# Joining the 64-row matmuls of two FFN parts, with five PSUM banks in one pool, in an mLSTM cell followed by a squared-ReLU FFN

## The chip, the cores and the metric

One core of one Trainium2 chip. The metric is the device time of one execution in microseconds (us). All runs quoted here are of the fast state; the records show a granted TensorE clock of 0.988 to 0.991 over the span. A 2% change of the time counts as faster or slower.

## The reference

```python
# attention: mLSTM cell, batch 4, 8 heads, 768 steps, head size 40
for t in range(S):
    m_new = np.maximum(f_gate[:, :, t] + m, i_gate[:, :, t])
    f_stab = np.exp(f_gate[:, :, t] + m - m_new)
    i_stab = np.exp(i_gate[:, :, t] - m_new)
    C = f_stab * C + i_stab * einsum('bhd,bhe->bhde', vt, kt)
    n = f_stab * n + i_stab * kt
    y[:, :, t] = sigmoid(o_gate) * (C @ qt) / maximum(abs(n . qt), 1)
# FFN on x = (3072 tokens, 320): w_in (320, 2048), w_out (2048, 320)
h = np.maximum(x @ w_in, 0.0)
out = h * h @ w_out
```

The kernel computes attention in tiles of 128 steps (24 tiles) and the FFN in groups of 256 tokens (12 groups). The FFN's first product has a contraction of 320 rows: 128 + 128 + 64.

## The kernel before

An FFN group is done in four parts. Each part makes four blocks of 128 hidden columns: sixteen 128-row matmul instructions (an f32 matmul stands as two instructions in the trace), then eight 64-row ones. The latter come in pairs, one in rows 0 to 63 of the array and one in rows 64 to 127, each pair writing two different banks.

```python
    ps_at = ctx.enter_context(tc.tile_pool(name="ps_at", bufs=3, space=PSUM))
    ps_h = ctx.enter_context(tc.tile_pool(name="ps_h", bufs=3, space=PSUM))
    ps_o = ctx.enter_context(tc.tile_pool(name="ps_o", bufs=2, space=PSUM))
    ...
    def ffn1(g, pp):
        ...
        hs = [ps_h.tile([P, 2, WG], F32, name="h_ps") for _ in range(2)]
        for i in range(2):
            for n in range(2):
                fb = 4 * pp + 2 * n + i
                for a in range(2):
                    nc.tensor.matmul(                                        # line 460, 128 rows
                        hs[i][:, n, :], lhsT=w_in[:, a, fb * P : (fb + 1) * P], rhs=xT[:, a, :],
                        start=(n == 0 and a == 0), stop=False,
                    )
        for n in range(2):
            for i in range(2):
                rows = slice(i * KR, (i + 1) * KR)                           # KR = 64
                nc.tensor.matmul(                                            # line 467, 64 rows
                    hs[i][:, n, :], lhsT=w_in2[rows, 2 * pp + n, :], rhs=xT[rows, 2, :],
                    start=False, stop=(n == 1),
                )
        st["half"] = hs, ...
    ...
    for n, (which, g, i) in enumerate(parts):    # which 1: first product of group g, part i
        s, at = 6 + n // 4, n % 4                # which 2: second product of group g, step i
        if at == 0:
            do(score, s)          # scores of tile s: 40-row matmuls in pairs, then P_sb on VectorE
        if at == 1:
            attend_on(s)          # hi, dC, hp on TensorE, then x_sb on VectorE
        ...
        if at == 3:
            do(turn_rows, s)      # x_sb -> xT
            do(transposes, s + 1) # k, q -> kT (copied by ScalarE), qT
        if which == 1:
            ffn1(g, i)
            relu_half()           # ScalarE, PSUM -> r_sb
            square_half()         # VectorE, r_sb -> g2
        elif g == 0:
            ffn2(g, *divmod(i, 2))
        else:
            ffn2_fast(g, i)       # two banks X and Y over four steps
        ...
        if at == 2:
            do(weigh_on, s + 1)   # ScalarE: eight exponentials of the next tile (line 325)
```

Sets of four of `which` 1 and 2 take turns, so each tile of attention goes with one set. In line numbers below, L460, L467, L547 and so on are of the kernel before; in the changed kernel the same lines stand a little lower (L461, L472, L555).

## Time and profile before

| | kernel before |
|---|---|
| time, median | 584.4 us (583.93 to 585.96, 3 runs; a fourth, later, makes it 584.85) |
| span of the profiled run | 582.2 us |
| TensorE busy | 98% |
| VectorE, ScalarE, GpSimd busy | 54%, 34%, 17% |
| 64-row matmuls (L467) | 384 instructions, 48 blocks of 8 |

A row of the page's costliest groups gives line, engine, operation, tile written and read, shapes, count, busy time and the mean of one instruction, then the idle time of that engine just before. Here are the two rows of the 64-row block: its matmuls and its weight loads.

```profile
L467 PE MATMUL h_ps<-xT,w_in 64*128 64x256 f32 x384 | 54.5, 402 | 0.0
L467 PEld LDWEIGHTS h_ps<-xT,w_in 64*128 64x128 f32 x384 | 33.1, 186 | 18.0 <-issue 15.2
```

The matmul row has no idle time before it at all, yet the weight-load row has 18 us, 15.2 of it "issue", that is, waiting for nothing the profile shows. This is how lost time looks on a TensorE that counts as busy: a matmul record lasts longer (0.38 us for the 256 columns) than the distance to the next start (0.216), so the later start after a change of shape (0.309) leaves no gap between matmul records, and only the weight loads show one, 0.33 us each time. That gap marks the place and is not the price: from start to start the way into a block costs 0.20 us (0.309 + 0.320 against 2 x 0.216).

### The profile page before, as it was taken

The numbers are of one execution on the slowest core, as the hardware profiler recorded it, in microseconds if no ns is written. First come the engines' busy times: TensorE is split into PE (matmuls) and PEld (weight loads), VectorE is DVE, ScalarE is ACT, GpSimd is POOL, SyncE is SP. The second block draws the span as 40 slices with busy tenths as digits, with TensorE's granted clock in tenths as the row PEclk, the third lists the DMA queues.
The fourth block names the chain that finished last, engine by engine and source line by source line (L and its number), as shares of the span: only waits on it lengthen the run. The fifth ranks groups of instructions, "written<-read, shape, count | busy, mean of one in ns | idle before, by whom it ended". The sixth has DMA issues, their size and how long they took to land.

```text
span 582.2 us, 9724 instructions
## 1 busy us (share of the span) xinstructions
PE 567.7 (98%) x3878; PEld 497.6 (85%) x3879; DVE 312.9 (54%) x602; ACT 197.6 (34%) x486; POOL 97.0 (17%) x113
## 2 busy tenths in 40 slices
PE   9988899969999999999999999999999999999997
PEld 5876788857789989989988988988987998988997
DVE  8689988656374364353364365355365355334441
ACT  3868665351333223414213415204225213112000
POOL 3455433132012020101110220100210200000000
PEclk9998999979999999999999999999999999999999
DMA  9997997822124233321431432141321000000000
GB/s 195 224 210 157 162 199 163 166 70 46 47 46 76 66 47 64 77 46 46 95 45 38 88 64 59 36 92 37 46 61 36 1 24 2 1 24 0 24 24 23
DMA packets 130909, 42.60 MB, mean 73 GB/s; under 512 B 101072, under 2 KB 127696, under 8 KB 130864
## 3 DMA queue, kind: packets, MB, share of 16 engines
q1 hardware_dynamic: 130768, 41.79, 34.7%
q8 instruction: 30, 0.49, 0.4%
q10 hardware_dynamic: 96, 0.20, 0.1%
q14 instruction: 15, 0.12, 0.1%
HBM read 37.95 MB, written 4.03 MB: 72 GB/s over the span
## 4 chain that ended last, share of the span: by engine, by line
PE 89%; DVE 6%; ACT 2%; issue 1%; POOL 1%; POOLq 0%; DVEq 0%; ACTq 0%
PE o_ps L547 29%; PE h_ps L460 26%; PE h_ps L467 8%; PE hp L399 6%; PE tp L362 4%; PE o_ps L493 3%; PE tp L349 3%; PE hi L385 3%; PE dC L392 3%; DVE mag L197 1%; PE tp L444 1%; ACT W_sb L325 1%; DVE mag L198 1%; PE idle L615 1%; PE A_ps L301 1%
## 5 line engine op out<-in xcount | busy, mean ns | idle before, releaser
L460 PE MATMUL h_ps<-xT,w_in 128*128 128x256 f32 x768 | 177.9, 385 | 1.1 <-ACT xT L445 1.1
L460 PEld LDWEIGHTS h_ps<-xT,w_in 128*128 128x128 f32 x768 | 143.0, 191 | 24.4 <-issue 4.0
L486 DVE TENSOR_TENSOR g<-r_sb 128x512 f32<-128x512 f32 x96 | 64.8, 716 | 90.4 <-ACT r_sb L479 90.4
L479 ACT ACTIVATE r_sb<-h_ps 128x512 f32<-128x512 f32 x96 | 52.0, 593 | 175.0 <-PE h_ps L467 174.6
L547 PE MATMUL o_ps<-w_out,g 128*128 128x160 f32 x528 | 76.9, 302 | 0.0
L547 PEld LDWEIGHTS o_ps<-w_out,g 128*128 128x128 f32 x528 | 72.5, 190 | 1.3 <-issue 0.3
L325 ACT ACTIVATE W_sb<-A_bc,b_T 128x128 f32<-128x128 f32 x176 | 53.8, 390 | 6.4 <-POOL A_bc L310 6.4
L467 PE MATMUL h_ps<-xT,w_in 64*128 64x256 f32 x384 | 54.5, 402 | 0.0
L547 PE MATMUL o_ps<-T,S 128*128 128x160 f32 x352 | 51.6, 300 | 0.0
L547 PEld LDWEIGHTS o_ps<-T,S 128*128 128x128 f32 x352 | 49.0, 190 | 0.1
L467 PEld LDWEIGHTS h_ps<-xT,w_in 64*128 64x128 f32 x384 | 33.1, 186 | 18.0 <-issue 15.2
L336 POOL TENSOR_TENSOR vw<-va,W_sb 128x328 f32<-128x328 f32 x20 | 15.4, 768 | 191.7 <-ACT W_sb L325 186.7
L399 PE MATMUL hp<-va,P_sb 128*128 128x41 f32 x368 | 44.1, 281 | 0.0
L399 PEld LDWEIGHTS hp<-va,P_sb 128*128 128x128 f32 x368 | 42.9, 192 | 0.0
L563 DVE TENSOR_TENSOR y_sb<-y_sb,o_ps 128x160 f32<-128x160 f32 x33 | 10.6, 321 | 55.1 <-PE o_ps L547 55.1
L418 POOL TENSOR_TENSOR C_sb<-C_sb,Cd 128x328 f32<-128x328 f32 x16 | 14.4, 898 | 132.9 <-DVE C_sb L410 132.8
L374 DVE TENSOR_TENSOR P_sb<-tp,W_sb 128x512 f32<-128x512 f32 x46 | 29.5, 684 | 12.3 <-PE tp L362 11.7
L563 DVE TENSOR_TENSOR y_sb<-o_ps,y_sb 128x160 f32<-128x160 f32 x22 | 7.1, 325 | 53.9 <-PE o_ps L547 31.1
L362 PEld LDWEIGHTS tp<-qT,kT 40*128 40x128 f32 x384 | 25.0, 195 | 11.8 <-ACT kT L353 7.1
L362 PE MATMUL tp<-qT,kT 40*128 40x128 f32 x384 | 28.5, 290 | 6.7 <-ACT kT L353 5.1
L572 ACT COPY y_sb<-o_ps 128x160 f32<-128x160 f32 x11 | 3.2, 292 | 70.8 <-PE o_ps L547 70.8
L349 PE MATMUL tp<-ident,kq 128*128 128x128 f32 x192 | 25.1, 274 | 1.6 <-DVE num L405 1.6
(98 smaller groups left out, 674.5 us busy)
## 6 DMA issues: line engine op xcount, KB each, us to landing
A_bc<-a_rows SPq DMA_DIRECT2D x22, 512.0 KB, 4.2
raw<-in_moe_w_out_dram SPq DMA_DIRECT2D x16, 320.0 KB, 3.3
raw<-in_moe_w_in_dram SPq DMA_DIRECT2D x8, 512.0 KB, 5.7
kq<-in_k_dram SPq DMA_DIRECT2D x24, 160.0 KB, 4.2
kq<-in_q_dram SPq DMA_DIRECT2D x24, 160.0 KB, 4.8
va<-in_v_dram SPq DMA_DIRECT2D x24, 160.0 KB, 4.1
og<-in_o_gate_dram SPq DMA_DIRECT2D x24, 160.0 KB, 3.9
out_dram<-y_sb SPq DMA_DIRECT2D x24, 160.0 KB, 1.8
```

What stands on the lines that cost most here:

```text
L325: nc.scalar.activation(d["W"][:, i * n + h, :], A[i][:, h, :], AF.Exp, bias=b_T[:, b, c, i * n + h : i * n + h + 1],)
L349: nc.tensor.transpose(tp[:, j, :], d["kq"][:, i, 2 * j : 2 * j + 2, :].rearrange("p h d -> p (h d)"), ident[:],)
L362: nc.tensor.matmul(sc[i][:, j, :], lhsT=d["kT"][rows, j, :], rhs=d["qT"][rows, j, :], start=True, stop=True,)
L374: nc.vector.tensor_tensor(t, d["sc"][i], d["W"][:].rearrange("p (j two) t -> p j two t", two=2)[:, :, i, :], op=ALU.mult,)
L385: nc.tensor.matmul(hi[:, 2 * j : 2 * j + 2, :].rearrange("p h d -> p (h d)"), lhsT=d["qT"][:, j, :], rhs=C[:, j].rearrange("p h d -> p (h ...
L399: nc.tensor.matmul(hp[:, h, :], lhsT=d["P"][h % 2][:, h // 2, :], rhs=d["va"][:, h, :], start=True, stop=True,)
L460: nc.tensor.matmul(hs[i][:, n, :], lhsT=w_in[:, a, fb * P : (fb + 1) * P], rhs=xT[:, a, :], start=(n == 0 and a == 0), stop=False,)
L467: nc.tensor.matmul(hs[i][:, n, :], lhsT=w_in2[rows, 2 * pp + n, :], rhs=xT[rows, 2, :], start=False, stop=(n == 1),)
L479: nc.scalar.activation(rs[-1][:], h[:], AF.Relu)
L486: nc.vector.tensor_tensor(g4[:, :, i, :], r[:], r[:], op=ALU.mult)
L547: nc.tensor.matmul(to, lhsT=lhsT[:, p], rhs=rhs[:, p, :], start=(start and p == 0), stop=(p == NPAIR - 1), skip_group_check=True,)
L563: add = lambda to, a, b: nc.vector.tensor_tensor(to, a, b, op=ALU.add)
```

## The change

The intent is to go to the 64-row shape half as often: the 64-row matmuls of parts 0 and 1 are issued together after part 1's 128-row ones, those of parts 2 and 3 after part 3's. Two parts are then open at once and hold four banks. As the FFN's first product had three banks and the second product two, the two pools become one of five, in tile 7, before the fourth group (group 3). The relus and squares of the first part of a pair move behind the joined block with those of the second.

```diff
+    banks = ExitStack()
+    ps_h = banks.enter_context(tc.tile_pool(name="ps_h", bufs=3, space=PSUM))
+    ps_o = banks.enter_context(tc.tile_pool(name="ps_o", bufs=2, space=PSUM))
...
-    def ffn1(g, pp):
+    def ffn1_main(g, pp):
...                                            # the 128-row matmuls, unchanged
+    def ffn1_rest(g, pp, hs):
...                                            # the 64-row matmuls, unchanged
+    def ffn1(g, pp):
+        ffn1_main(g, pp)
+        ffn1_rest(g, pp, st["half"][0])
...
-            st["o_ps"] = ps_o.tile([P, W], F32, name="o_ps")[:, :DM]
+            st["o_ps"] = ps_h.tile([P, W], F32, name="h_ps")[:, :DM]
...                                            # X and Y of ffn2_fast likewise from ps_h (no longer swapped by g)
         if n == 4:
             ...
+            banks.close()
+            ps_h = ctx.enter_context(tc.tile_pool(name="ps_h", bufs=5, space=PSUM))
...
-        if which == 1:
+        if which == 1 and g < 3:
             ffn1(g, i)
             relu_half()
             square_half()
+        elif which == 1:
+            ffn1_main(g, i)
+            if i % 2 == 0:
+                held = st["half"]
+            else:
+                both = held, st["half"]
+                for more, half in enumerate(both):
+                    ffn1_rest(g, i - 1 + more, half[0])
+                for half in both:
+                    st["half"] = half
+                    relu_half()
+                    square_half()
```

More of the change, by code (lines that the diff above doesn't have):

```diff
@@ L80 @@
     ps_at = ctx.enter_context(tc.tile_pool(name="ps_at", bufs=3, space=PSUM))
-    ps_h = ctx.enter_context(tc.tile_pool(name="ps_h", bufs=3, space=PSUM))
-    ps_o = ctx.enter_context(tc.tile_pool(name="ps_o", bufs=2, space=PSUM))
+    banks = ExitStack()
+    ps_h = banks.enter_context(tc.tile_pool(name="ps_h", bufs=3, space=PSUM))
+    ps_o = banks.enter_context(tc.tile_pool(name="ps_o", bufs=2, space=PSUM))
     ctx.enter_context(tc.manual_schedule())
@@ L463, in ffn1 @@
                     )
+        st["half"] = hs, st["g2", g][:, 4 * pp : 4 * pp + 4, :].rearrange("p (n two) t -> p n two t", two=2)
+    def ffn1_rest(g, pp, hs):
+        xT = st["xT", g]
         for n in range(2):
@@ L470, in ffn1 @@
                 )
-        st["half"] = hs, st["g2", g][:, 4 * pp : 4 * pp + 4, :].rearrange("p (n two) t -> p n two t", two=2)
+    def ffn1(g, pp):
+        ffn1_main(g, pp)
+        ffn1_rest(g, pp, st["half"][0])
     def relu_half():
@@ L554, in ffn2_fast @@
         if step == 0:
-            banks = [ps_o.tile([P, W], F32, name="o_ps") for _ in range(2)]
-            st["o2"] = banks[:: 1 if g % 2 else -1], [ffn.tile([P, DM], F32, name="y_sb") for _ in range(2)]
+            st["o2"] = [ps_h.tile([P, W], F32, name="h_ps") for _ in range(2)], [ffn.tile([P, DM], F32, name="y_sb") for _ in range(2)]
         (X, Y), (y0, y1) = st["o2"]
@@ L752 @@
         if which == 2 and g >= NG - 3 and g + 1 < NG and i == 3:
-            for k in (1, 2, 3):
-                sums(g + 1, slice(0, NPAIR), (k,))
+            for one in (1, 2, 3):
+                sums(g + 1, slice(0, NPAIR), (one,))
         if at == 3:
```

## The prediction

> **What bounds the kernel now.** I read the page's busy row first, then the PE's waits, then the chain of work that ended last. The busy row and the slices:
>
> ```profile
> span 582.2 us, 9724 instructions
> PE 567.7 (98%) x3878; PEld 497.6 (85%) x3879; DVE 312.9 (54%) x602; ACT 197.6 (34%) x486; POOL 97.0 (17%) x113
> ...
> PE   9988899969999999999999999999999999999997
> ```
>
> TensorE is busy 98% of the span, and from slice 11 on nothing else can set the end: the other engines are at most about half busy there. The list of what PE waited for holds only 11.2 us in all, and its two large entries (5.1 us for kT, at 121.7 to 126.7 us, and the waits of the start) lie before the place where the change begins. So PE's waits are not where a gain can come from, or hardly; what is left is how densely PE's own instructions follow each other. For that I read the chain, whose pieces are laid end to end. Columns: start, length, what, how many instructions.
>
> ```profile
> 299.83 1.73 PE h_ps L460 x8
> 301.56 1.06 PE h_ps L467 x8
> 302.62 3.65 PE h_ps L460 x16
> 306.27 1.06 PE h_ps L467 x8
> 307.34 0.48 PE tp L444 x3
> 307.82 0.87 PE tp L349 x8
> 308.69 3.46 PE h_ps L460 x16
> ```
>
> L460 are the 128-row matmuls of an FFN part (16 instructions), L467 its 64-row ones (8 instructions, two at a time in the two halves of the array). Look at the same L460 x16: 3.46 us after a transposition, 3.65 us directly after a 64-row block. A clean pitch is 1.73/8 = 0.216 us. Eight 64-row instructions of the same 256 columns, two side by side, should be four pitches, 0.864 us; they take 1.06. Each crossing between the two shapes costs something, in both directions.
>
> ```profile
> 330.91 0.33 PE tp L444 x3
> ...
> 339.03 1.06 PE h_ps L467 x8
> 340.10 1.05 PE hi L385 x8
> 341.15 0.89 PE dC L392 x8
> ```
>
> The followers of a block show the same: L444 x3 takes 0.48 us after a 64-row block, 0.33 after 128-row products; L385 takes 1.05 us after a block where its twin L392 takes 0.89.
>
> **What the Trainium skill says.** TensorEngine Tiling (Array Packing), section Key Properties: "Changing tiling mode (not just tile) drains the TensorE". The trace agrees: the start of the first 64-row matmul is 0.309 us after the last 128-row one and the second pair 0.320 us after the first, where 0.216 is the pitch in the middle of the block; on the way out it is 0.306 and 0.320. TensorE: Matmul & The Clock Gate, section The mechanism (Part 3), says that matmuls in different row tiles overlap; here the two of a pair start 0.006 to 0.007 us apart. TensorEngine Tiling, section Gotcha 1: PSUM Pressure, says that different row tiles cannot use one PSUM bank at once, which is why each part needs two banks, and holding two parts open needs four. Perfetto Trace Analysis, section on the Tensor Engine Instruction, says that matmul ends are computed and not observed, so I count from start to start, or with differences of like pieces.
>
> **The change, part by part.** It touches groups 3 to 11, nine groups of four parts. In each, the 64-row block of part 0 is put behind part 1's 128-row matmuls and joined to part 1's block, and the same for parts 2 and 3. The listing of instructions by engine confirms it: 128-row x8 (source matmuls), attention, 128-row x8, then 64-row x8 in one run; no matmul is added or removed.
>
> What one joined pair saves is one whole visit to the 64-row shape, by what followed the removed block:
> - The block itself: 1.06 - 4 x 0.216 = 0.196 us, every time.
> - Follower L385 or L392 (part 0, groups 3 to 10): 1.05 - 0.89 = 0.16. Together 0.36 us x 8 = 2.9 us. Single starts give 0.309+0.758+0.306+0.175 = 1.548 against 0.864+0.216+0.112 = 1.192, the same 0.356.
> - Follower L444 (part 2, groups 3 to 10): 0.48 - 0.33 = 0.15. Together 0.35 us x 8 = 2.8 us.
> - Follower L460 (parts 0 and 2 of group 11, where attention is over): 3.65 - 3.46 = 0.19. Together 0.39 us x 2 = 0.8 us.
> Sum: 6.5 us for 18 visits. All of it lies on PE, which sets the end, with no gap to swallow it. The entry and exit at the remaining 18 blocks stay, and the 64-row score matmuls behind part 3 stay in the same shape as before.
>
> A second gain comes from ScalarE's order. Before, the relus of part 2 stand ahead of the exponentials of the next tile (L325), and those ahead of the copy of kT that the scores need:
>
> ```profile
> 176.04 1.13 PE L467 MATMUL h_ps<-xT,w_in 64*128 64x256 f32 x8
> ...
> 176.54 0.58 ACT L353 COPY kT<-tp 128x512 f32<-128x512 f32 x1
> ...
> 177.17 1.16 PE L362 MATMUL tp<-qT,kT 40*128 40x128 f32 x16
> ...
> 178.27 0.95 PE L547 MATMUL o_ps<-w_out,g 128*128 128x160 f32 x5
> ```
>
> Here kT ends at 177.12 and the scores start at 177.17, 1.13 us after the block began; in the groups without an activation-table load the same distance is 0.97 (493.87 to 494.84) and the scores then take 0.99 instead of 1.10. So a small wait of 0.27 us hides inside, in 4 of the 9 groups. After the change the relus of part 2 come behind kT, the exponentials can start about 4 us earlier, and the wait should go: 4 x 0.27 = 1.1 us.
>
> The pool of five banks: per cycle two banks for the output products and eight for four parts, ten in all, so the rotation repeats. X is bank 0 and Y bank 1; the first two parts take 2, 3, 4, 0, the next two 1, 2, 3, 4. The tightest return is bank 2: it is wanted when the second half of part 2's 128-row matmuls starts, 8 x 0.216 + 0.1 = 1.8 us after the joined block. Its relu may start 0.4 us after part 0's last 64-row matmul, which is about 1.2 us before the block's end, and takes 0.55 us: free 0.2 us before the block ends, 2 us to spare. The other three relus end by 1.4 us after the block. Y's bank is wanted after the scores (1.0) and 16 products (2.2), its relu also done before. I expect no wait. The switch of pools at the fourth group costs at most a wait for the last two relus: they ended at 127.65, the first product stood at 128.75, so nothing.
>
> Sum: 6.5 + 1.1 = 7.6 us, less nothing: 584.4 - 7.5 = 576.9 us.
>
> **Rivals.**
> (a) A bank wait takes the place of the drain. Four relus in a row (4 x 0.55 us) and four squares (4 x 0.65 us) now come at once, and if ScalarE is in other work when they fall due, PE stands at bank 2 or at Y. For it: fewer banks are free at any time, and ScalarE is in order. Against: it waited 174.6 us in all for L467 to give it relu work, 7.2 us at 302.65 alone. If it held at every pair for 0.4 us, the gain would be gone: 584.
> (b) The squares delay what VectorE owes attention: P_sb for the hp products, the adds that free the output banks. Behind part 3, I reckon the last square 2.5 us after the block, P_sb at 3.8, hp wanted at 7.2: slack of 3 us. Against (b) also: VectorE waits 90.4 us for relus now. If wrong, 0.5 us in nine groups, 577 becomes 581.
> (c) The extra time at a crossing belongs not to the change of shape but to the block, for example to the first pair's weights having to be loaded in view, so that each part pays it even in a joined run. Then only the exit is saved: about half, 3.2 us, and 580 with the second gain. Against: inside today's blocks all pairs but the first run at 0.216.
> (d) The second gain does not come because the exponentials wait for their mask rather than for ScalarE: 578.
>
> **Range and chances.** The arithmetic of the crossing is from starts that repeat within 0.002 us over nine groups, so the main doubt is a new wait (a, b), which only makes it slower, and the scatter of the times before (583.93 to 585.96). I put 80% on 575.4 to 579.6. 2% would be 11.7 us: more than every crossing that the change removes is worth. Faster by over 2%: 0.03; within: 0.96; slower: 0.01.
>
> **What would show it right or wrong.** Right: the 64-row line has 18 runs of x16 in groups 3 to 11, each about 1.93 us in the chain (1.06 + 4 x 0.216); L444 and L385 behind 128-row matmuls are back at 0.33 and 0.89; PE busy falls by about 6.5 us; the four distances of 1.13 between block and scores are gone; the list of PE's waits has nothing new on relus. Wrong: PE idle before L461 or the second output product, released by ScalarE's relu or VectorE (a, b); joined runs of 2.1 us (c); or a granted clock below 0.99 from the denser stream.

## The result

The changed kernel's time is 576.65 us in the median (575.94 to 578.51, 4 runs), the kernel before 584.85 us (4 runs). The ratio is 0.9864, with a 95% interval of 0.9833 to 0.9894. A ratio here is the mean time of one kernel's fast runs over that of the other's fast runs of the same rounds, so not quite the ratio of the medians quoted. This is a gain of 1.4%.

The busy rows of the changed kernel's page:

```profile
span 575.8 us, 9736 instructions
PE 560.6 (97%) x3879; PEld 501.9 (87%) x3879; DVE 313.2 (54%) x602; ACT 196.4 (34%) x486; POOL 98.3 (17%) x113
```

PE's busy time fell by 7.1 us (567.7 to 560.6) and its share even by a point, although no matmul was taken away. Perfetto Trace Analysis of the Trainium skill, section Identifying the Most-Contended Engine, warns of this: matmul busy share is not a good measure of how close TensorE is to its limit. This trace agrees: 98% busy before, and yet 1.4% could be gained by issuing the same matmuls in another order.

The chain of the changed kernel over one group (group 3), where the prediction showed the same kinds of pieces before (start, length, what, instructions):

```profile
157.23 1.07 PE h_ps L467 x8
158.30 1.05 PE hi L385 x8
...
170.24 1.06 PE h_ps L467 x8
171.30 0.48 PE tp L444 x3
...
176.11 1.06 PE h_ps L467 x8
177.17 0.00 issue
177.17 1.16 PE tp L362 x16
```

That was the kernel before; this is the changed one:

```profile
155.24 3.65 PE h_ps L461 x16
158.89 0.85 PE hi L386 x8
...
165.92 1.93 PE h_ps L472 x16
...
171.50 0.33 PE tp L445 x3
...
176.15 1.93 PE h_ps L472 x16
178.08 0.89 PE tp L363 x16
```

Two blocks of 8 took 2.12 to 2.13 us; one of 16 takes 1.93. The followers of the removed blocks are back at their clean lengths: hi 0.85 instead of 1.05, the three transpositions 0.33 instead of 0.48. And the scores at the end of the group follow their block without the "issue" piece and take 0.89 instead of 1.16: the small wait for kT is gone. The timeline of the changed kernel shows why. ScalarE was idle before the relus, instead of just done with kT:

```profile
176.08 2.00 PE L472 MATMUL h_ps<-xT,w_in 64*128 64x256 f32 x16
177.25 2.06 ACT L487 ACTIVATE r_sb<-h_ps 128x512 f32<-128x512 f32 x4 [3.46 <-PE h_ps L472]
177.88 2.50 DVE L494 TENSOR_TENSOR g<-r_sb 128x512 f32<-128x512 f32 x4 [4.45 <-ACT r_sb L487]
177.91 1.06 PE L363 MATMUL tp<-qT,kT 40*128 40x128 f32 x16
```

Last, what the weight loads of the 64-row block waited for, in the view of that source line (cause, us in all, times), before and after:

```profile
  issue: 15.2, 46
```

```profile
  issue: 9.3, 28
```

There are 18 gaps fewer, 5.9 us in all, 0.33 us each: their number is that of the 18 visits to the 64-row shape that the change takes away. What a visit costs is another figure (0.40 us, below), for it has a way in and a way out.

**A measure that scatters less than the time.** The start of the kernel, up to about 127 us, varies from run to run by more than a microsecond (the profiled run of the changed kernel was its slowest, 578.51 us, and reached tile 7 at 128.28 us, where a later run of the same kernel reached it at 126.95; from 60 to 90 us the clock granted was 0.94 in the first and 1.00 in the second). The change begins only after that. So the experiments are compared on the tail, from the first score matmul of tile 7 to the end of the span: 455.5 us before, 447.5 changed. The stretch of tile 7 itself still scatters by 0.45 us (25.68 to 26.13; from 127 to 152 us the clock granted was 0.86 to 0.91), so the table below has also the tail from tile 8's scores on; that one repeated within 0.01 us, and from 154 to 570 us every profile shows a granted clock of 1.00.

### The profile page after: what moved, and what is told of

The parts are those of the page before. It is cut to its first block, busy times and chain, and to the rows that moved or that the text cites. A ratio compares the mean times of both kernels' runs of the same rounds, so it can differ in the third digit from the quotient of the medians.

```text
span 575.8 us, 9736 instructions
## 1 busy us (share of the span) xinstructions
PE 560.6 (97%) x3879; PEld 501.9 (87%) x3879; DVE 313.2 (54%) x602; ACT 196.4 (34%) x486; POOL 98.3 (17%) x113
## 4 chain that ended last, share of the span: by engine, by line
PE 88%; DVE 6%; ACT 2%; issue 1%; POOL 1%; DMA 1%; SPq 0%; POOLq 0%; DVEq 0%; ACTq 0%
PE h_ps L555 29%; PE h_ps L461 27%; PE h_ps L472 7%; PE hp L400 6%; PE tp L363 4%; PE tp L350 3%; PE h_ps L501 3%; PE hi L386 3%; PE dC L393 2%; DVE mag L198 1%; ACT W_sb L326 1%; PE tp L445 1%; DVE mag L199 1%; DMA kq<-in_q_dram 1%; PE A_ps L302 1%
## 5 line engine op out<-in xcount | busy, mean ns | idle before, releaser
L487 ACT ACTIVATE r_sb<-h_ps 128x512 f32<-128x512 f32 x96 | 50.1, 600 | 171.6 <-PE h_ps L472 171.6
L494 DVE TENSOR_TENSOR g<-r_sb 128x512 f32<-128x512 f32 x96 | 62.2, 704 | 75.3 <-ACT r_sb L487 75.3
L555 PE MATMUL h_ps<-w_out,g 128*128 128x160 f32 x528 | 76.9, 302 | 0.0
L555 PEld LDWEIGHTS h_ps<-w_out,g 128*128 128x128 f32 x528 | 72.5, 190 | 1.3 <-ACT r_sb L487 0.3
L555 PE MATMUL h_ps<-T,S 128*128 128x160 f32 x352 | 51.4, 299 | 0.0
L472 PE MATMUL h_ps<-xT,w_in 64*128 64x256 f32 x384 | 49.6, 392 | 0.0
L555 PEld LDWEIGHTS h_ps<-T,S 128*128 128x128 f32 x352 | 49.0, 190 | 0.0
L569 DVE TENSOR_TENSOR y_sb<-y_sb,h_ps 128x160 f32<-128x160 f32 x33 | 10.6, 321 | 55.1 <-PE h_ps L555 55.1
L569 DVE TENSOR_TENSOR y_sb<-h_ps,y_sb 128x160 f32<-128x160 f32 x22 | 7.1, 324 | 49.6 <-PE h_ps L555 30.9
L350 PE MATMUL tp<-ident,kq 128*128 128x128 f32 x192 | 27.0, 286 | 3.7 <-DVE num L406 3.2
L578 ACT COPY y_sb<-h_ps 128x160 f32<-128x160 f32 x11 | 3.2, 292 | 70.6 <-PE h_ps L555 63.9
```

Source lines behind the costliest of these rows:

```text
L350: nc.tensor.transpose(tp[:, j, :], d["kq"][:, i, 2 * j : 2 * j + 2, :].rearrange("p h d -> p (h d)"), ident[:],)
L472: nc.tensor.matmul(hs[i][:, n, :], lhsT=w_in2[rows, 2 * pp + n, :], rhs=xT[rows, 2, :], start=False, stop=(n == 1),)
L487: nc.scalar.activation(rs[-1][:], h[:], AF.Relu)
L494: nc.vector.tensor_tensor(g4[:, :, i, :], r[:], r[:], op=ALU.mult)
L555: nc.tensor.matmul(to, lhsT=lhsT[:, p], rhs=rhs[:, p, :], start=(start and p == 0), stop=(p == NPAIR - 1), skip_group_check=True,)
L569: add = lambda to, a, b: nc.vector.tensor_tensor(to, a, b, op=ALU.add)
```

## The experiments

All eight kernels gave correct results. Each was timed in three rounds beside the kernel before; the first four ran on one chip (where the kernel before had a median of 585.24 us), the last four on another (585.27).

| kernel | time, median us | ratio to before | tail from tile 7 | tail from tile 8 |
|---|---|---|---|---|
| before | 584.85 | 1 | 455.49 | 429.80 |
| changed | 576.65 | 0.9864 | 447.54 | 421.74 |
| pool only | 585.80 | 1.0001 | 455.38 | 429.63 |
| relus late | 584.17 | 0.9975 | 454.49 | 428.53 |
| first pair joined | 581.94 | 0.9938 | 451.92 | 426.04 |
| second pair joined | 580.25 | 0.9917 | 451.13 | 425.33 |
| two visits a part | 598.05 | 1.0218 | 469.00 | 442.88 |
| scores in the joined block | 572.44 | 0.9785 | 443.72 | (moved) |
| four banks | 576.56 | 0.9853 | 447.71 | 421.75 |
| changed, again | 576.70 | 0.9855 | 447.52 | 421.74 |

The argument rests on the tails.

My theory: a visit to the 64-row shape costs TensorE 0.35 to 0.40 us beyond its matmuls, each joined pair saves one visit, and ScalarE's new order takes away four small waits for kT. Rivals: the freer banks do it; the cost goes with the part and not with the visit; the second gain is only a by-product of the joined blocks.

### The pool alone

```diff
-        if which == 1 and g < 3:
+        if which == 1:
```

> Only the pool of five banks; every part keeps its own 64-row block. Measured on the tail, from the first score matmul of tile 7 to the end of the span (before 455.5 us, changed kernel 447.5). Theory (a visit to the 64-row shape costs 0.35 to 0.40 us, a late kT 0.27 us in four groups, the pool only the two waits of 0.095 us at the last group boundaries): tail 455.3, time as before, within 0.1%. Rival (the freer banks are what gains, the joining only comes along): tail near 448, time 1.3% lower.

Measured: tail 455.38 us, ratio 1.0001 (0.9977 to 1.0024). From tile 8 the tail is 0.17 us shorter than before. That is where the second products of two groups follow each other at the end of the kernel, shown by the timeline of the kernel before and then of this one:

```profile
550.40 2.43 PE L547 MATMUL o_ps<-T,S 128*128 128x160 f32 x16
```

```profile
550.62 2.34 PE L555 MATMUL h_ps<-T,S 128*128 128x160 f32 x16
```

The same sixteen matmuls take 0.09 us less, and this happens twice (0.19 us). The likely reason, which no view names, is that with two banks Y of the next group waits for the last add that reads the same bank, and with five it finds another. The pool makes the change possible and is itself worth almost nothing.

### The relus late, the blocks where they were

```diff
-            ffn1_main(g, i)
+            ffn1(g, i)
             if i % 2 == 0:
                 held = st["half"]
             else:
                 both = held, st["half"]
-                for more, half in enumerate(both):
-                    ffn1_rest(g, i - 1 + more, half[0])
```

> The 64-row blocks stay where they were; only the relus and squares of each first part are put off to its second part, as in the changed kernel. Theory: the four waits for kT go (4 x 0.27 = 1.1 us), nothing else: tail 455.3 - 1.1 = 454.2, the four distances of 1.13 us between block and scores become 0.97. Rival (the small gain of ScalarE's order is in truth a by-product of the joined blocks): tail 455.3.

Measured: from tile 8 the tail is 428.53, which is 1.10 us under the pool alone; from tile 7 it is 454.49 (0.3 above the expectation, all of it in tile 7's own stretch, 25.96 us here). The block with its own eight instructions now has its scores on time; compare 176.04, 177.17 and 178.27 in the prediction's last fence:

```profile
177.75 1.13 PE L472 MATMUL h_ps<-xT,w_in 64*128 64x256 f32 x8
178.72 1.06 PE L363 MATMUL tp<-qT,kT 40*128 40x128 f32 x16
178.92 1.09 ACT L487 ACTIVATE r_sb<-h_ps 128x512 f32<-128x512 f32 x2 [3.38 <-PE h_ps L472]
179.71 1.49 PE L555 MATMUL h_ps<-w_out,g 128*128 128x160 f32 x9
```

From the block's start to the scores it is 0.97 us (before: 1.13), from the scores to the products 0.99 (1.10): 0.27 us in each of four groups. So the second gain needs no joined block; it comes with the later relus and squares alone. What went is PE's wait for kT, a copy on ScalarE, and ScalarE's queue now has the exponentials and that copy ahead of the relus of part 2. The four groups are those in which ScalarE also loads an activation table ahead of the exponentials (1.28 us, at 172.44, 262.44, 354.23 and 444.24 us in the kernel before).

### Each pair alone

```diff
-        if which == 1 and g < 3:
+        if which == 1 and (g < 3 or i >= 2):   # first pair joined; (g < 3 or i < 2) for the second
```

> Parts 0 and 1 joined, parts 2 and 3 as before. Nine visits fewer, eight of them followed by hi or dC (0.40 us each, as the comparison of the two traces gives) and one by L461 (0.40); the relus of part 2 still stand before the exponentials, so the kT waits stay. Theory: tail 455.3 - 3.6 = 451.7. If the relus' order were the main cause: 455.

> Parts 2 and 3 joined, parts 0 and 1 as before. Nine visits fewer (8 x 0.35 + 0.40 = 3.2 us) and the kT waits gone (1.1 us). Theory: tail 455.3 - 4.3 = 451.0. The gains of this run and of the first-pair run should add up to that of the changed kernel (8.0 us, the pool's 0.2 counted once). If the gain needs both pairs (say by the rotation of banks), they do not add up.

Measured from tile 8, against the pool alone (429.63): the first pair 3.59 us, the second pair 4.30 us. Together 7.89; the changed kernel has 429.63 - 421.74 = 7.89. The two halves add up exactly, so neither needs the other. The first-pair kernel also keeps what the theory says it must keep. Its chain has the joined block of parts 0 and 1, the unjoined block of part 3, and the wait before the scores:

```profile
164.88 1.93 PE h_ps L472 x16
...
176.33 1.06 PE h_ps L472 x8
177.40 0.00 issue
177.40 1.16 PE tp L363 x16
```

In the second-pair kernel the scores take 0.89 us, as in the changed one, and hi behind part 0's block still takes 1.05.

### Two visits for each part

The opposite direction: the same matmuls, with the two halves of each part's 64-row matmuls behind the 128-row matmuls they belong to.

```diff
+        for n in range(2):
             for i in range(2):
-                for n in range(2):
-                    ...                        # 128-row matmuls
-        for n in range(2):
+                ...                            # 128-row matmuls of this n
             for i in range(2):
                 ...                            # 64-row matmuls of this n
```

(The pool is the five-bank one, nothing is joined, and groups 0 to 2 are as before.)

> The opposite direction: the pool of five, no joining, and each part of groups 3 to 11 goes to the 64-row shape twice, with half of its 64-row matmuls each time: 36 visits more, each from and to 128-row matmuls (0.40 us). The same matmuls otherwise. Theory (cost by the visit): tail 455.3 + 36 x 0.40 = 469.7, or 468.6 if the later scores take away the kT waits. Rival (cost by the part, or by the 64-row matmuls themselves): tail 455.3.

Measured: tail 469.00 us, ratio 1.0218 (1.0191 to 1.0245). None of the 1.13 us distances is left, as the scores now come later than kT. From tile 8: 442.88 - 429.63 = 13.25, plus the 1.10 that the vanished kT waits are worth, is 14.35 us for 36 more visits: 0.399 us each. The expectation had 0.40. The chain of one part:

```profile
203.19 1.92 PE h_ps L490 x8
205.11 0.63 PE h_ps L496 x4
205.74 1.92 PE h_ps L490 x8
207.66 0.63 PE h_ps L496 x4
208.30 1.05 PE hi L386 x8
```

Two blocks of 4 take 1.26 us where one of 8 takes 1.06, and each run of eight 128-row matmuls takes 1.92 where 1.73 is clean. The cost goes by the visit; the rival of a cost by the part or by the 64-row matmuls themselves falls. (The 1.10 us is taken over from the kernel with late relus; without it the 36 visits come to 0.368 us each.)

### The scores in the joined block

In the sets with a first product, the scores of the tile ahead of part 0 were still a visit of their own. Here they move into the joined block of parts 0 and 1; attention's products follow part 2, and the rows are turned after part 3.

```diff
+        late_score = which == 1 and g > 2 and s < NT
-        if at == 0:
+        if at == 0 and not late_score:
             do(score, s)
-        if at == 1:
+        if at == 1 and not late_score:
             attend_on(s)
...
         if at == 3:
-            do(turn_rows, s)
+            if not late_score:
+                do(turn_rows, s)
...
                 held = st["half"]
+                if late_score and i == 2:
+                    attend_on(s)
             else:
+                if late_score:
+                    (score if i == 1 else turn_rows)(s)
                 both = held, st["half"]
```

> The changed kernel, and in groups 3 to 10 the score matmuls of the tile, which were a visit to the 64-row shape of their own ahead of part 0, move to the joined block of parts 0 and 1; attention's products follow part 2's 128-row matmuls, and the rows are turned after part 3's. Eight visits fewer, each 0.093 + 0.101 + 0.090 + 0.104 = 0.39 us by the single starts. Theory: tail 447.5 - 3.1 = 444.4, and about 0.5% off the changed kernel's time. Rival (P_sb, x_sb or the output banks come too late in the new order): waits of PE for VectorE appear and the tail stays at 447 or above.

Measured: 572.44 us in the median, ratio to before 0.9785 (0.9762 to 0.9809), tail 443.72 us. Against the changed kernel run on the same chip (mean of fast runs 572.64 against 576.85) that is 0.7% less time. The chain of one group, with no wait in it:

```profile
152.26 6.91 PE h_ps L461 x32
159.17 1.09 PE tp L363 x16
160.26 1.73 PE h_ps L472 x16
161.99 3.65 PE h_ps L461 x16
...
173.82 1.93 PE h_ps L472 x16
175.75 0.89 PE tp L363 x16
```

The entry into the shape is now paid by the scores (1.09 instead of 0.89), and the sixteen 64-row matmuls behind them take 1.73 us, eight clean pitches. PE's list of waits is that of the kernel before, 11.2 us, all of it before tile 8; neither P_sb nor x_sb came late. The expectation of 444.4 was short of the gain: 3.8 us instead of 3.1. In the seven cycles of two tiles that can be compared one by one, each saves 0.44 us where I had reckoned 0.39. The other 0.05 us is in the chains: the sixteen 128-row matmuls of part 1 took 3.53 us behind hp and take 3.46 now (half of 6.91), while the eight L350 behind hp take 0.90 instead of 0.87. The remaining 0.3 us is in the stretch of tile 7.

### Four banks

```diff
-            ps_h = ctx.enter_context(tc.tile_pool(name="ps_h", bufs=5, space=PSUM))
+            ps_h = ctx.enter_context(tc.tile_pool(name="ps_h", bufs=4, space=PSUM))
```

> The changed kernel with four banks in the pool, not five, so two open parts hold all of it. By the clearance reckoned in the prediction the first relu of a pair is done before the next part needs its bank, so theory: tail 447.5, no wait of PE for a relu, within 0.3 us. Rival (five banks are needed, as the change has them): waits of about 0.5 us in 18 places, tail 455 or more.

Measured: 576.56 us, tail from tile 8 421.75, that is, the changed kernel's to 0.01 us. The list of PE's waits names no relu. Its largest three entries (line waited, releaser, us, times, longest):

```profile
PE tp L363 <- ACT kT L354: 5.1, 1, 5.1
PE tp L363 <- ACT qT L354: 1.6, 1, 1.6
PE tp L350 <- DVE num L406: 1.6, 2, 1.0
```

All of these lie before tile 8, where the joined parts begin, and stand in the kernel before as well; from there on the list is empty. So the change does not need the fifth bank in the shared pool; that bank is free for another use. It just fits: in this trace the first relu of parts 0 and 1 ends 0.17 us before part 2's first matmul starts in its bank, in all nine groups (whether two separate pools could do it was not tried).

### The changed kernel again

> The changed kernel once more, unaltered, beside the others on this chip: tail 447.5 again within 0.2 us, if that measure repeats; the time 1.2 to 1.6% under the kernel before.

Measured: 576.70 us, ratio 0.9855 (0.9835 to 0.9875), tail 447.52 and from tile 8 421.74, the same as in the first profile to 0.02 us. Every stretch between two tiles' scores from tile 8 on repeated within 0.01 us. This is what allows differences of 0.2 us to be read from single profiles here, from tile 8 on.

## Why the prediction was right

**The bound.** It held: TensorE set the end before and after. From tile 8 on its waits for other engines did not matter, but for the four of 0.27 us for kT, which the list of waits does not show and which the prediction found in the timeline.

**The price of a visit (6.5 us for 18).** Right in mechanism and nearly in size. The two pairs alone give 3.59 and, less the 1.10 of kT, 3.20: 6.79 us. The difference of 0.3 us is one term: for the follower of part 0 I took L392 (0.89 us) as the clean length of L385, because no L385 follows L460 in the trace before. In the changed kernel it takes 0.85 there, that is 0.04 us less in eight groups. The trace before had this figure already: at 318.64 us L385 takes 0.85 us behind other 128-row matmuls (L547). The reverse experiment puts 0.399 us on a visit between 128-row matmuls of the first product, where the prediction had 0.39.

**The second gain (1.1 us).** Right: 1.10 us by the kernel with late relus alone. The exponentials started 4.6 us earlier against the start of part 2's 128-row matmuls (before: 302.55 to 308.34; changed: 301.02 to 302.18), the prediction said about 4. Rival (d), that they would wait for their mask, falls.

**The pool.** "I expect no wait" was right, and that the switch of pools costs nothing too. What the step left out is a gain: 0.19 us by the two waits at the last group boundaries. One of the readings on banks is wrong: a part needs two banks because its four blocks of 256 columns fill two tiles of two blocks, whichever rows compute them; the rule on row tiles bears only on which blocks share a bank. And I did not conclude that four banks would do. With four the 2 us to spare are gone, as part 2 wants its first bank right after the block; what is left is the 0.2 us that I had reckoned between the first relu's end and the block's end, and the four-bank trace has 0.17.

**The sum.** 7.6 us predicted; from tile 8 on 8.06 us measured (429.80 to 421.74): 6.79 for the visits, 1.10 for kT, 0.17 for the pool. 576.9 us predicted, 576.65 measured. That the two times lie 0.25 us apart is partly luck: the prediction took off 7.5 where its sum was 7.6, and started from a median of 584.4 that a fourth run moved to 584.85; the gain itself was 0.46 us larger than the sum.

**The rivals.** (a) A bank wait: none. (b) Late squares: in the changed kernel a joined block ends at 311.33, the last square at 313.62, P_sb at 314.82, and hp is wanted at 318.51, so 2.3, 3.5 and 7.2 us after the block where the prediction had 2.5, 3.8 and 7.2. (c) A price by the block: against it are the 1.93 us of the joined blocks and the 1.73 us of a block behind scores. The two-visits kernel does not decide this, since there each visit is also a block. The sign of a clock below 0.99: the profiled run has 0.988, but not from the denser stream, as its low stretches lie before tile 8 or after the last matmul (1.00 from 154 to 570 us) and the kernel before has runs at 0.988 too (586.05 us beside the pool kernel).

**What stays open.** That the array drains at a change of shape is the account of the Trainium skill (TensorEngine Tiling (Array Packing), section Key Properties); the runs show the price and that it goes with the change of shape, not its inside. A weight load that cannot run ahead of the change would fit as well: in the timeline before, the first 64-row weight load starts together with its matmul (both at 301.49 us). No run separates the two.

## What to carry to other kernels

When TensorE is busy nearly all the span and waits for nothing, look at the same line behind different neighbours in the chain: 3.46 against 3.65 us for the same sixteen matmuls is what gave the cost away. Count how often the stream changes between full-row and half-row matmuls, price one change from start to start, and put all half-row work (here also the 40-row scores) next to each other as far as PSUM banks allow; check the number of banks by when the first reader ends and when the bank is wanted next, not by how many tiles are open. And see what else the reordering moves: here a seventh of the gain came from relus that had stood ahead of other work in ScalarE's queue.

## What the Trainium skill lacked or had wrong

- TensorEngine Tiling (Array Packing), section Key Properties: says that changing the tiling mode drains TensorE, and gives no price. Here a visit from 128-row to 64-row f32 matmuls and back costs 0.39 us from start to start (0.309 + 0.320 us in, 0.306 + 0.320 out, where 0.216 is the pitch), and by 36 added visits 0.399 us each.
- The same page: lists 64-row tiles for contractions of up to 64 rows, but does not say outright that matmuls of 64 and of 40 rows can follow each other without a change of mode. Here the 40-row scores follow a 64-row block after 0.209 us, the usual pitch of the block, and sixteen 64-row matmuls behind scores take 1.73 us, without any entry price.
- No page says how such a drain looks in a profile: the matmul rows show 0.0 us of idle time, and only the weight-load row has a gap, 0.33 us a time under "issue" (15.2 us in 46, and 9.3 us in 28 after the change). The gaps count the visits; their length is not the price of 0.40 us.
- TensorEngine Tiling, section Gotcha 1: PSUM Pressure, says that row tiling raises the pressure on PSUM, but gives no way to size a pool; no run here shows that row tiling took more banks. Two open parts of two banks each, with two more for the second product, ran in a pool of four at the speed of five (421.75 and 421.74 us).
